# Moving 38 on-chip transposes from TensorE to the DMA queue in a layernorm, linear attention and SwiGLU kernel

## The chip, the cores and the metric

The kernel runs on one core of a Trainium2 chip. The metric is the device time of one execution in microseconds (us); 306.36 us is the median of the three runs shown for the kernel before. Engines are named as in the profile: PE (TensorE, matrix multiply; PEld is its weight load), ACT (ScalarE), DVE (VectorE), POOL (GpSimd), SP (SyncE, which here does nothing but issue DMAs).

## What is computed

S = 2048 tokens of D = 640 features, 32 heads of 20 features, F = 1536. Everything is bfloat16 at the borders.

```python
xn = _layernorm(x, axis=-1)
return x + _A_ref(xn, A_wqkv, A_w_phi, A_wo) + _B_ref(xn, B_w1, B_w3, B_w2)

# _A_ref
q, k, v = qkv[0], qkv[1], qkv[2]                  # from x @ wqkv
pq = jnp.einsum("bhsd,hdf->bhsf", q, w_phi)
pk = jnp.einsum("bhsd,hdf->bhsf", k, w_phi)
phi_q = jnp.concatenate([_softmax(pq, axis=-1), _softmax(-pq, axis=-1)], axis=-1)
phi_k = jnp.concatenate([_softmax(pk, axis=-1), _softmax(-pk, axis=-1)], axis=-1)
kv = jnp.einsum("bhsf,bhsd->bhfd", phi_k, v)
z  = jnp.einsum("bhsf->bhf", phi_k)
num = jnp.einsum("bhqf,bhfd->bhqd", phi_q, kv)
den = jnp.einsum("bhqf,bhf->bhq", phi_q, z)[..., None] + 1e-6
o = num / den                                     # then (B, S, D) @ wo

# _B_ref
h = _silu(gate) * up                              # gate = x @ w1, up = x @ w3
out = jnp.einsum("bsf,fd->bsd", h, w2)
```

## The kernel before

The tokens are cut into T = 16 tiles of 128, and into 4 blocks of 512 for the products that keep 512 tokens in the free dimension. A matmul contracts over the 128 partitions, so the features must lie on the partitions: DC = 5 chunks of 128 make up D. All operands stay in SBUF.

The steps, by the names in the code and the tiles that the profile shows:

- `loads` issues all early DMAs on SP, in one list: token tiles into `x_tok`, `wv`, the k part and the q part of `wqkv` into `wqk_s`, `phi_s`, and `w1_s`, `w3_s` in three slices each (the profile calls these two and `w2_s` `w_s`).
- `ln_stats` (DVE BN_STATS and BN_AGGR, then POOL for the power -0.5) and `ln_apply` (DVE or ACT) normalise `x_tok` in place. `xn_transpose` turns one tile: five PE transposes (matmuls against `ident`, seen as `PS<-ident,x_tok`) into one PSUM bank, and one copy by ACT or DVE into `xnT`.
- `fold_t` transposes one 128-column strip of wk or wq in the same way (`PS<-ident,wqk_s`, five per strip, five strips per weight) into `wqkT`; `fold_mm` multiplies it with the block diagonal of w_phi (`BDc`) into `Wkp` or `Wqp`, so that no separate feature-map product is needed later. One call of `fold_mm` is six matmuls.
- `v_tile` and `k_tile` are ten matmuls of 320 columns each per token tile; `k_tile` is followed by two exponentials on ACT into `ekt`. `k_norm` divides them by their sums: a sum and a reciprocal on DVE (`S64`, `rS64`), two multiplications on POOL, which write `ekt` again.
- `kv_sum` sums over all 16 token tiles: ten groups of 16 matmuls (`PS<-v,ekt`), each followed on DVE and POOL by the masking into `KVc`. It needs the last `k_norm`.
- `q_proj` (five matmuls of 512 columns and two exponentials into `EqT`), then `q_tok` per token tile: 12 matmuls against `KVc`, two small ACT copies, and six DVE operations up to `o_tok`, which has three buffers. `o_transpose` turns `o_tok` into `oT`: five PE transposes (`PS<-ident,o_tok`) and a copy.
- `mlp` is one of 48 units (4 blocks of 12): ten matmuls of 512 columns, a tanh on ACT, two DVE operations (`t1`, `hT`). `out_tile` is 34 matmuls of 320 columns per token tile (`wo_s`, `w2_s`), an addition on DVE (`xres`), and a store.

The order is set by a planner that runs when the program is built. Six streams (`norms`, `attention`, `k_norms`, `o_transposes`, `mlps`, `outs`) each offer their next step; for each the planner works out from its own costs when the step could start, and takes the earliest. What it takes is appended to the lists of the engines, and at run time each engine goes through its list in order, waiting on semaphores. So a step that was planned for a certain moment holds up everything behind it on the same engine if its data come later. The steps of `attention` win ties over those of `mlps`. A DMA in the plan holds SP for 0.06 us and moves at a fixed rate.

Parts of SBUF are used twice: `hT3` and `w2_s` lie on `ekt`, so block 3 of `mlps` waits in the plan until `kv_sum` is done; `hT2` lies on `x_tok`; `oT` lies on `v2`; `KVc`, `prod` and `o_tok` lie on `wqkT`.

The comparison that picks the next step:

```python
            if any(o.eng == "PE" for o in ops):
                at = max(P.ready(ops), P.free["PE"] + 0.15)
            else:
                at = P.start_of(ops[0])
                if i == 0 and at < P.free["PE"] + 2.0:
                    at = -1.0
            if best is None or at < best[0]:
                best = (at, i, ops, after)
```

Of the kernel before, what the change touches and what calls it, by code (L numbers as in the profile page):

```python
# [9 lines left out]
D = 640  # L10
# [4 lines left out]
DC = D // 128  # L15
# [27 lines left out]
class _Program:  # L43
# [60 lines left out]
        self.pending.append(o)  # L104
        return o

    def dma(self, eng, out, in_):
        m = self.eng[eng].dma_start
        nbytes = 1
        for n in out.shape:  # L110
            nbytes *= n
        nbytes *= mybir.dt.size(out.dtype)
        o = _Op(eng, lambda: m(out, in_), self.regions(in_), self.regions(out), nbytes, True)  # L113
        o.name = "dma:" + out.name
        self.pending.append(o)
        return o
# [123 lines left out]
def bass_parallel_sum__linear_kernel_hedgehog__glu_gated_swiglu__prompt_kernel(  # L240
# [11 lines left out]
    bf = DT.bfloat16  # L252
    f32 = DT.float32
    P = _Program(nc)
# [6 lines left out]
    def region(size):  # L261
        o = top[0]
        top[0] = o + (size + 31) // 32 * 32
        assert top[0] <= arena_size, top[0]
        return a0 + o

    def new(name, shape, dtype, offset=None):
        size = mybir.dt.size(dtype)
        for n in shape[1:]:
            size *= n  # L270
        return P.sbuf(name, shape, dtype, region(size) if offset is None else offset)
# [15 lines left out]
    xnT = new("xnT", [128, DC, S], bf)  # L287
# [8 lines left out]
    x_tok = new("x_tok", [128, T, D], bf, RX)  # L296
# [12 lines left out]
    RE = region(40960)  # L309
# [1 line left out]
    hT3 = new("hT3", [128, FC, 512], bf, RE)  # L311
    w2_s = new("w2_s", [128, FC, D], bf, RE + 12288)
    EqT1 = new("EqT1", [128, 2, DC, 512], bf, RE + 27648)
    wqk_s = new("wqk_s", [128, DC, 2 * D], bf, RE + 40960 - 12800)
    hT = [hT0, hT1, hT2, hT3]

    RV = region(21504)
# [1 line left out]
    oT = new("oT", [128, DC, S], bf, RV)  # L319
# [4 lines left out]
    wqkT = new("wqkT", [128, 2 * DC, D], bf, RW)  # L324
    KVc = new("KVc", [128, 2, DC, 8 * 22], bf, RW)
    prod = new("prod", [128, 2, 2, D], bf, RW + 3520)
    o_tok = new("o_tok", [128, 3, D], bf, RW + 8640)
# [3 lines left out]
    PSb = PS[:].bitcast(bf)  # L331
# [14 lines left out]
    def tr(o, i, idn=None):  # L346
        idn = ident[:] if idn is None else idn
        P.op("PE", "transpose", [o], [i, idn], (o, i, idn), cost=0.06)

    def free(ap):  # L350
        n = 1
        for s in ap.shape[1:]:
            n *= s
        return n
# [13 lines left out]
    def copy(eng, o, i, fast=1):  # L368
        if eng == "ACT":
            act(o, i, ACT.Copy)  # L370
        else:
            P.op(eng, "tensor_copy", [o], [i], (o, i), cost=0.14 + free(o) / 960 / fast)

    def evac(o, i):

        a = P.free["ACT"] + 0.17 + free(o) / 1200
        d = P.free["DVE"] + 0.14 + free(o) / 960 / (2 if i.dtype == bf else 1)
        copy("ACT" if a <= d else "DVE", o, i, 2 if i.dtype == bf else 1)
# [12 lines left out]
    wqkv_t = A_wqkv.rearrange("(c p) n -> p c n", p=128)  # L391
# [4 lines left out]
    def loads():  # L396
        def x(a, b):
            P.dma("SP", x_tok[:, a:b, :], x_t[:, a:b, :])

        def w13(a, b):  # L400
            P.dma("SP", w1_s[:, :, a:b], w1_t[:, :, a:b])
            P.dma("SP", w3_s[:, :, a:b], w3_t[:, :, a:b])

        x(0, 1)
        x(1, 2)
        P.dma("SP", wv[:], wqkv_t[:, :, 2 * D:3 * D])
        x(2, 4)
        P.dma("SP", wqk_s[:, :, D:2 * D], wqkv_t[:, :, D:2 * D])
        P.dma("SP", phi_s[:], phi_t)
        x(4, 8)  # L410
        w13(0, 512)
        x(8, 12)
        P.dma("SP", wqk_s[:, :, 0:D], wqkv_t[:, :, 0:D])
        w13(512, 1024)
        x(12, 16)
        w13(1024, 1536)
# [40 lines left out]
    def xn_transpose(t, k):  # L457
        for dc in range(DC):
            tr(PSb[:, k * 1024 + 128 * dc:k * 1024 + 128 * dc + 128],
               x_tok[:, t, 128 * dc:128 * dc + 128])  # L460
        src = PSb[:, k * 1024:k * 1024 + D].rearrange("p (c n) -> p c n", n=128)
        evac(xnT[:, :, t * 128:(t + 1) * 128], src)


    def block_diag():
        for c in range(DC):
# [2 lines left out]
            tt("POOL", BDc[:, c, 0:n * DH].rearrange("p (h k) -> p h k", k=DH),  # L469
               phi_s[:, c, :].unsqueeze(1).to_broadcast([128, n, DH]),  # L470
               GM[:, c, h0:h1 + 1].unsqueeze(2).to_broadcast([128, n, DH]), ALU.mult)

    def fold_t(which, e, k):
        for dc in range(DC):
            tr(PSb[:, k * 1024 + 128 * dc:k * 1024 + 128 * dc + 128],
               wqk_s[:, dc, which * D + 128 * e:which * D + 128 * e + 128])
        evac(wqkT[:, which * DC + e, :], PSb[:, k * 1024:k * 1024 + D])

    def fold_mm(which, dc, k):
        first = [True, True]  # L480
# [92 lines left out]
           g.unsqueeze(3).to_broadcast([128, 4, 16, DH]), ALU.mult)  # L573
        tt("DVE", o_tok[:, t % 3, :], p2[:, 0, :], p2[:, 1, :], ALU.add, 2)

    def o_transpose(t, k):
        for dc in range(DC):
            tr(PSb[:, k * 1024 + 128 * dc:k * 1024 + 128 * dc + 128],
               o_tok[:, t % 3, 128 * dc:128 * dc + 128])
        src = PSb[:, k * 1024:k * 1024 + D].rearrange("p (c n) -> p c n", n=128)  # L580
        evac(oT[:, :, t * 128:(t + 1) * 128], src)


    nmlp = [0]

# [13 lines left out]
    def load_xres(t):  # L599
        P.dma("SP", xres[:, t % 4, :], x_t[:, t, :])  # L600
# [15 lines left out]
    def banks(n):  # L616

        def free_at(k):
            return max([o.end for i in range(k, k + n) for o in P.bank.get(("P", i), {}).values()],
                       default=0.0)  # L620
        return min(range(0, 8, n), key=free_at)
# [33 lines left out]
    def transposed(t):  # L655
        while done["ln"] <= t:
            yield None
        yield lambda: xn_transpose(t, banks(1))
        done["t"] = t + 1

    def attention():
        yield from transposed(0)
        for t in range(4):
            if t < 3:
                yield from transposed(t + 1)
            yield lambda t=t: v_tile(t, banks(2))
        for e in range(DC):
            yield lambda e=e: fold_t(1, e, banks(1))
        for dc in range(DC):
            yield lambda dc=dc: fold_mm(1, dc, banks(2))  # L670
        for t in range(T):
            yield lambda t=t: k_tile(t, banks(2))
            done["k"] = t + 1
            if 2 <= t < 14:
                yield from transposed(t + 2)
            if t >= 4:
                yield lambda t=t: v_tile(t, banks(2))
            if 4 <= t < 9:
                yield lambda e=t - 4: fold_t(0, e, banks(1))
            if 9 <= t < 14:  # L680
                yield lambda dc=t - 9: fold_mm(0, dc, banks(2))
        yield lambda: P.dma("SP", wo_s[:], A_wo.rearrange("(c p) d -> p c d", p=128))
        for fc in range(DC):
            yield lambda fc=fc: q_proj(0, fc, banks(1))
        while done["n"] < T:
            yield None
        for fc in range(DC):
            for sg in range(2):
                yield lambda fc=fc, sg=sg: kv_sum(sg, fc, banks(1))
        done["kv"] = 1  # L690
        yield lambda: P.dma("SP", w2_s[:], B_w2.rearrange("(c p) d -> p c d", p=128))
        yield lambda: (load_xres(0), load_xres(1))
        for b in range(NB):
            for j in range(4):
                t = 4 * b + j
                yield lambda t=t: q_tok(t, banks(4))
                done["q"] = t + 1
                if b + 1 < NB:
                    for fc in range((5 * j + 3) // 4, (5 * j + 8) // 4):
                        yield lambda b=b, fc=fc: q_proj(b + 1, fc, banks(1))  # L700

    def o_transposes():
        for t in range(T):
            while done["q"] <= t:
                yield None
            yield lambda t=t: o_transpose(t, banks(1))
            done["o"] = t + 1

    def mlps():
# [14 lines left out]
    n = len(streams)  # L724
    heads, alive = [None] * n, [True] * n
    while any(alive):
        best = None
        for i in range(n):
            if heads[i] is None and alive[i]:
                s = next(streams[i], StopIteration)  # L730
                if s is StopIteration:
                    alive[i] = False
                else:
                    heads[i] = s
            if heads[i] is None:
                continue
            save = nmlp[0], len(finish)
            ops = P.step(heads[i])
            after = nmlp[0], finish[save[1]:]
            nmlp[0] = save[0]  # L740
            del finish[save[1]:]
            if any(o.eng == "PE" for o in ops):
                at = max(P.ready(ops), P.free["PE"] + 0.15)
            else:
                at = P.start_of(ops[0])
                if i == 0 and at < P.free["PE"] + 2.0:
                    at = -1.0
            if best is None or at < best[0]:
                best = (at, i, ops, after)
        if best is None:  # L750
            continue
        at, i, ops, after = best
        nmlp[0] = after[0]
        finish.extend(after[1])
        P.commit(ops)
        heads[i] = None
# [61 lines left out]
```

## Time and profile before

| what | value |
|---|---|
| time, three runs | 305.68, 306.36, 308.53 us; median 306.36 us |
| time of the profiled execution | 307.55 us |
| span of its instructions | 305.8 us (1.75 us of the time lie around it) |
| PE | 286.2 us busy, 94% of the span, 2066 matmuls |
| DVE, ACT, POOL | 191.6, 118.4, 59.1 us busy |
| mean granted TensorE clock | 0.988 of full speed |

The span is the time from the first to the last instruction on the chip. Matmuls overlap in the profile, since their ends are modelled: the time that a group really takes is the distance from its start to the start of the next group on PE, and not its own duration. The share of busy time is a mean over stages with different limits, so the rows further below go stage by stage.

### The profile page before, as it was taken

The page shows a single profiled execution, that of the slowest core. Times are in us where ns is not written, and L with a number is a line of the kernel's source. Part 1 is how long each engine was busy: PE and PEld are TensorE (multiplying, and loading weights), DVE is VectorE, ACT ScalarE, POOL GpSimd, SP SyncE. Part 2 cuts the span into 40 slices and gives each one's busy share as a digit, 9 for nine tenths or more (in the row PEclk, how much of TensorE's full clock was granted, in tenths as well). Part 3 has the DMA queues.
Part 4 walks back from the last instruction along what each step waited for, and adds up shares of the span by engine and source line. Part 5 has one row for each costly group of instructions (what it writes and reads, how often), then busy time and mean ns, then how long its engine had stood idle before and what let it go on. Part 6 is the DMA issues. An engine that isn't in the chain of part 4 may idle for free.

```text
span 305.8 us, 4978 instructions
## 1 busy us (share of the span) xinstructions
PE 286.2 (94%) x2066; PEld 181.9 (59%) x2066; DVE 191.6 (63%) x335; ACT 118.4 (39%) x212; POOL 59.1 (19%) x90
## 2 busy tenths in 40 slices
PE   0699999999999999999659999999999999999995
PEld 0476777775444444444359555555667777777773
DVE  3758888889566656565734699799546675511212
ACT  2277989868522232323100565556323311200000
POOL 4431646898800000000061000000000000000000
PEclk9999999999999999999968999999999999999999
DMA  7998000030000000000000810000101221122121
GB/s 230 340 355 260 2 1 2 1 109 0 2 0 0 0 2 0 1 2 0 0 0 2 263 62 0 2 1 2 43 0 45 58 73 45 61 70 86 43 66 43
DMA packets 15543, 17.38 MB, mean 57 GB/s; under 512 B 1441, under 2 KB 15521, under 8 KB 15521
## 3 DMA queue, kind: packets, MB, share of 16 engines
q1 hardware_dynamic: 15520, 17.07, 17.5%
q8 instruction: 16, 0.26, 0.4%
q14 instruction: 7, 0.05, 0.1%
HBM read 14.44 MB, written 2.62 MB: 56 GB/s over the span
## 4 chain that ended last, share of the span: by engine, by line
PE 92%; DVE 3%; DMA 2%; POOL 1%; ACT 1%; issue 0%; SPq 0%
PE PS L101 92%; DMA x_tok<-in_A_x_dram 2%; POOL ekt L101 1%; DVE prod L101 0%; DVE S_61 L101 0%; SPq L113 0%; ACT EqT_81 L101 0%; DVE bst L101 0%; DVE xres L101 0%; DVE t_68 L101 0%; ACT th L101 0%; DVE den_s L101 0%; DVE rS_62 L101 0%; DVE x_tok L101 0%; ACT e_s L101 0%
## 5 line engine op out<-in xcount | busy, mean ns | idle before, releaser
L101 PE MATMUL PS<-xnT,w_s 128*128 128x512 bf16 x480 | 105.7, 379 | 0.0
L101 PEld LDWEIGHTS PS<-xnT,w_s 128*128 128x128 bf16 x480 | 46.4, 98 | 54.1 <-ACT EqT_75 L101 0.3
L101 ACT ACTIVATE th<-PS 128x512 f32<-128x512 f32 x48 | 28.8, 601 | 75.0 <-PE PS L101 75.0
L101 POOL TENSOR_TENSOR ekt<-ekt,rS_62 128x640 bf16<-128x640 bf16 x32 | 39.7, 1273 | 78.8 <-DVE rS_62 L101 78.7
L101 DVE SCALAR_TENSOR_TENSOR t_68<-th,PS 128x512 bf16<-128x512 f32 x48 | 32.9, 685 | 31.0 <-ACT th L101 30.9
L101 DVE TENSOR_TENSOR xres<-PS,xres 128x640 bf16<-128x640 f32 x16 | 13.2, 825 | 48.5 <-PE PS L101 48.5
L101 PE MATMUL PS<-wv,xnT 128*128 128x320 bf16 x160 | 26.3, 316 | 0.0
L101 PE MATMUL PS<-wo_s,oT 128*128 128x320 bf16 x160 | 24.6, 299 | 0.8 <-ACT EqT_81 L101 0.8
L101 DVE TENSOR_REDUCE S_61<-ekt 128x64 f32<-128x1280 bf16 x16 | 23.3, 1455 | 1.7 <-ACT ekt L101 1.7
L101 DVE TENSOR_TENSOR prod<-PS,g_s 128x1280 bf16<-128x1280 f32 x16 | 23.9, 1491 | 0.5
L101 PE MATMUL PS<-Wkp,xnT 128*128 128x320 bf16 x160 | 24.0, 299 | 0.0
L101 PE MATMUL PS<-xnT,Wqp 128*128 128x512 bf16 x100 | 23.7, 379 | 0.0
L101 ACT ACTIVATE ekt<-PS 128x640 bf16<-128x640 f32 x32 | 20.8, 705 | 7.2 <-PE PS L101 7.1
L101 ACT ACTIVATE e_s<-PS 128x64 f32<-128x64 f32 x32 | 9.1, 283 | 37.3 <-PE PS L101 36.3
L101 PEld LDWEIGHTS PS<-wv,xnT 128*128 128x128 bf16 x160 | 16.0, 104 | 6.2
L101 PEld LDWEIGHTS PS<-wo_s,oT 128*128 128x128 bf16 x160 | 15.1, 98 | 7.1 <-ACT EqT_81 L101 1.0
L101 PE MATMUL PS<-v_83,ekt 128*128 128x147 bf16 (+1 forms) x160 | 13.9, 259 | 5.7 <-POOL ekt L101 5.7
L101 DVE BATCH_NORM_STATS2 bst<-x_tok 128x6 f32<-128x320 bf16 x32 | 15.3, 477 | 5.6 <-DMA x_tok<-in_A_x_dram 5.0
L101 PEld LDWEIGHTS PS<-Wkp,xnT 128*128 128x128 bf16 x160 | 15.2, 98 | 5.3
L101 PEld LDWEIGHTS PS<-v_83,ekt 128*128 128x128 bf16 x160 | 13.5, 113 | 6.3 <-POOL ekt L101 6.0
L101 PE MATMUL PS<-ident,x_tok 128*128 128x128 bf16 x80 | 7.9, 236 | 9.4 <-DVE x_tok L101 9.4
L101 PEld LDWEIGHTS PS<-xnT,Wqp 128*128 128x128 bf16 x100 | 9.4, 98 | 8.8
(65 smaller groups left out, 325.1 us busy)
## 6 DMA issues: line engine op xcount, KB each, us to landing
w_s<-in_B_w_dram SPq DMA_DIRECT2D x6, 640.0 KB, 10.2
xres<-in_A_x_dram SPq DMA_DIRECT2D x16, 160.0 KB, 2.4
out_dram<-xres SPq DMA_DIRECT2D x16, 160.0 KB, 1.8
x_tok<-in_A_x_dram SPq DMA_DIRECT2D x3, 640.0 KB, 9.0
w_s<-in_B_w_dram SPq DMA_DIRECT2D x1, 1920.0 KB, 8.1
wqk_s<-in_A_wqkv_dram SPq DMA_DIRECT2D x2, 800.0 KB, 9.2
wv<-in_A_wqkv_dram SPq DMA_DIRECT2D x1, 800.0 KB, 5.9
wo_s<-in_A_wo_dram SPq DMA_DIRECT2D x1, 800.0 KB, 4.6
```

Source lines behind the costliest of these rows:

```text
L101: o = _Op(eng, lambda: m(*args, **kw), r, w, cost)
```

## The change

Three kinds of transposes leave PE and become DMAs with a transpose, issued by SP: those of the normalised token tiles 4 to 15 (`x_tok` to `xnT`, SBUF to SBUF), those of the attention output (`o_tok` to `oT`, SBUF to SBUF, all 16 tiles), and those of wk and wq, which are now read from DRAM straight into `wqkT` in one DMA of 800 KB each; `wqk_s` and `fold_t` are gone. Token tiles 0 to 3 are still transposed on PE. With each PE transpose goes its copy out of PSUM. Besides, steps of the stream `k_norms` are planned as if they could start 4 us earlier than they can.

```diff
-    def dma(self, eng, out, in_):
-        m = self.eng[eng].dma_start
+    def dma(self, eng, out, in_, transpose=False):
+        m = self.eng[eng].dma_start_transpose if transpose else self.eng[eng].dma_start
...
-        P.dma("SP", wqk_s[:, :, D:2 * D], wqkv_t[:, :, D:2 * D])
         P.dma("SP", phi_s[:], phi_t)
+        P.dma("SP", wqkT[:, DC:2 * DC, :], A_wqkv[:, D:2 * D], True)
         x(4, 8)
         w13(0, 512)
         x(8, 12)
-        P.dma("SP", wqk_s[:, :, 0:D], wqkv_t[:, :, 0:D])
+        P.dma("SP", wqkT[:, 0:DC, :], A_wqkv[:, 0:D], True)
...
-        yield lambda: xn_transpose(t, banks(1))
+        if t < 4:
+            yield lambda: xn_transpose(t, banks(1))
+        else:
+            yield lambda: P.dma("SP", xnT[:, :, t * 128:(t + 1) * 128], x_tok[:, t, :], True)
...
-        for e in range(DC):
-            yield lambda e=e: fold_t(1, e, banks(1))
...
-            if 4 <= t < 9:
-                yield lambda e=t - 4: fold_t(0, e, banks(1))
...
-            yield lambda t=t: o_transpose(t, banks(1))
+            yield lambda t=t: P.dma("SP", oT[:, :, t * 128:(t + 1) * 128], o_tok[:, t % 3, :], True)
...
                 at = P.start_of(ops[0])
+                if i == 2:
+                    at -= 4.0
```

The plan comes out in another order on every engine. Four places matter below.

First, PE behind the last `v_tile` of tiles 0 to 3 (`wv`). `PS<-ident,wqk_s` is `fold_t`, `PS<-BDc,wqkT` is `fold_mm`, `PS<-xnT,w_s` is `mlp`, `PS<-Wkp,xnT` is `k_tile`. Before:

```order
L101 MATMUL PS<-wv,xnT 128x320 x20
L101 MATMUL PS<-ident,wqk_s 128x128 x25
L101 MATMUL PS<-xnT,w_s 128x512 x10
L101 MATMUL PS<-BDc,wqkT 128x140 x2
L101 MATMUL PS<-BDc,wqkT 128x80 x2
L101 MATMUL PS<-BDc,wqkT 128x140 x4
```

And now:

```order
L101 MATMUL PS<-wv,xnT 128x320 x20
L101 MATMUL PS<-BDc,wqkT 128x140 x2
L101 MATMUL PS<-BDc,wqkT 128x80 x2
L101 MATMUL PS<-BDc,wqkT 128x140 x4
...
L101 MATMUL PS<-BDc,wqkT 128x140 x2
L101 MATMUL PS<-Wkp,xnT 128x320 x40
L101 MATMUL PS<-xnT,w_s 128x512 x50
```

The 30 matmuls of `fold_mm` now stand directly behind `wv`, with no unit of `mlp` between them and `k_tile`; the first five units come behind four `k_tile`.

Second, PE around `kv_sum` (`PS<-v,ekt`), behind the last `v_tile`. Before:

```order
L101 MATMUL PS<-wv,xnT 128x320 x10
L101 MATMUL PS<-xnT,Wqp 128x512 x25
L101 MATMUL PS<-xnT,w_s 128x512 x330
L101 MATMUL PS<-v_83,ekt 128x147 x64
L101 MATMUL PS<-v_83,ekt 128x168 x32
L101 MATMUL PS<-v_83,ekt 128x147 x64
```

And now:

```order
L101 MATMUL PS<-wv,xnT 128x320 x10
L101 MATMUL PS<-xnT,Wqp 128x512 x25
L101 MATMUL PS<-xnT,w_s 128x512 x10
L101 MATMUL PS<-v_82,ekt 128x147 x64
L101 MATMUL PS<-v_82,ekt 128x168 x32
L101 MATMUL PS<-v_82,ekt 128x147 x64
```

One unit of `mlp` stands ahead of `kv_sum` instead of 33; the others follow it, beside `q_tok`.

Third, SP, the queue of DMAs, up to the first store. Before:

```order
L113 DMA x_tok<-in_A_x_dram 128x2x640
L113 DMA wqk_s<-in_A_wqkv_dram 128x5x640
L113 DMA phi_s<-in_A_w_phi_dram 128x5x20
L113 DMA x_tok<-in_A_x_dram 128x4x640
L113 DMA w_s<-in_B_w_dram 128x5x512 x2
```

And now:

```order
L113 DMA phi_s<-in_A_w_phi_dram 128x5x20
L113 DMA_TRANSPOSE wqkT<-in_A_wqkv_dram 128x5x640
L113 DMA x_tok<-in_A_x_dram 128x4x640
...
L113 DMA w_s<-in_B_w_dram 128x5x512 x2
L113 DMA_TRANSPOSE xnT<-x_tok 128x5x128 x12
L113 DMA wo_s<-in_A_wo_dram 128x5x640
L113 DMA w_s<-in_B_w_dram 128x12x640
L113 DMA xres<-in_A_x_dram 128x640 x2
L113 DMA_TRANSPOSE oT<-o_tok 128x5x128 x16
```

The transposed wk stands ahead of token tiles 4 to 7; the 12 transposes of token tiles stand behind all early loads and ahead of those of `wo_s` and `w2_s`, the 16 of the attention output behind these.

Fourth, DVE and ACT while wk is folded. DVE (from the last statistics of tiles 4 to 7) and ACT (from the copies of the last two of the first four `v_tile`) before:

```order
L101 BN_AGGR mv<-bst 128x2
L101 COPY wqkT<-PS 128x640 x3
L101 SCALAR_TENSOR_TENSOR t_68<-th,PS 128x512
L101 SCALAR_TENSOR_TENSOR hT_76<-t_68,PS 128x512
...
L101 ACTIVATE v_83<-PS 128x32x20 x2
L101 ACTIVATE x_tok<-x_tok,rstd 128x640
L101 ACTIVATE wqkT<-PS 128x640 x2
L101 ACTIVATE th<-PS 128x512
L101 ACTIVATE x_tok<-x_tok,rstd 128x640
L101 ACTIVATE Wkp<-PS 128x640 x3
```

And now:

```order
L101 BN_AGGR mv<-bst 128x2
L101 CAST Wkp<-PS 128x640 x2
L101 TENSOR_SCALAR x_tok<-x_tok,mv,rstd 128x640
...
L101 ACTIVATE v_82<-PS 128x32x20 x2
L101 ACTIVATE x_tok<-x_tok,rstd 128x640
L101 ACTIVATE Wkp<-PS 128x640 x3
L101 ACTIVATE x_tok<-x_tok,rstd 128x640 x2
```

Two of the five copies into `Wkp` now stand on DVE directly behind the statistics of tiles 4 to 7, and three on ACT directly behind the `ln_apply` of tile 4; the copies into `wqkT` and the units of `mlp` that stood there are gone.

## Rows read from the trace of the kernel before

**Rows 1.** The page: the chain that ended last, by engine

```profile
PE 92%; DVE 3%; DMA 2%; POOL 1%; ACT 1%; issue 0%; SPq 0%
```

**Rows 2.** Stretches of 10 us: busy PE, PEld, DVE, ACT, POOL; clock; DMA

```profile
150.00:160.00 10.00, 4.30 (x39) 3.97 (x37) 5.41 (x9) 0.00 (x0) 5.32 (x6) 0.77 0.00 0
160.00:170.00 10.00, 10.00 (x124) 9.41 (x122) 3.99 (x16) 0.00 (x0) 1.73 (x8) 0.89 0.04 4
...
220.00:230.00 10.00, 8.64 (x77) 6.01 (x76) 6.00 (x10) 4.29 (x10) 0.00 (x0) 1.00 0.07 17
```

**Rows 3.** PE in order of time: start us, duration us, group

```profile
19.00 1.56 PE L101 MATMUL PS<-ident,wqk_s 128*128 128x128 bf16 x25
20.39 2.32 PE L101 MATMUL PS<-xnT,w_s 128*128 128x512 bf16 x10
...
57.12 0.48 PE L101 MATMUL PS<-BDc,wqkT 128*128 128x140 bf16 x6
57.43 1.52 PE L101 MATMUL PS<-Wkp,xnT 128*128 128x320 bf16 x10
58.79 0.44 PE L101 MATMUL PS<-ident,x_tok 128*128 128x128 bf16 x5
59.07 1.52 PE L101 MATMUL PS<-wv,xnT 128*128 128x320 bf16 x10
```

**Rows 4.** PE in order of time around the sum over keys

```profile
149.42 1.06 PE L101 MATMUL PS<-v_83,ekt 128*128 128x147 bf16 x14
153.96 0.24 PE L101 MATMUL PS<-v_83,ekt 128*128 128x147 bf16 x1 [3.48 <-POOL ekt L101]
156.41 12.59 PE L101 MATMUL PS<-v_83,ekt 128*128 128x147 bf16 x145 [2.21 <-POOL ekt L101]
```

**Rows 5.** DVE in order of time, late in the same stretch

```profile
168.00 0.30 DVE L101 TENSOR_TENSOR KVc<-PS,GM 128x140 bf16<-128x140 f32 x1 [0.51 <-PE PS L101]
...
169.04 0.30 DVE L101 TENSOR_TENSOR KVc<-PS,GM 128x140 bf16<-128x140 f32 x1 [0.51 <-PE PS L101]
```

**Rows 6.** The page: key normalise on POOL (busy us, mean ns | idle before, releaser)

```profile
L101 POOL TENSOR_TENSOR ekt<-ekt,rS_62 128x640 bf16<-128x640 bf16 x32 | 39.7, 1273 | 78.8 <-DVE rS_62 L101 78.7
```

**Rows 7.** DVE and ACT in order of time around the fold of wk

```profile
13.05 1.02 DVE L101 BATCH_NORM_STATS2 bst<-x_tok 128x6 f32<-128x320 bf16 x2 [0.17 <-DMA x_tok<-in_A_x_dram]
...
17.49 0.21 DVE L101 BATCH_NORM_AGGREGATE mv<-bst 128x2 f32<-128x12 f32 x1
...
19.80 0.91 ACT L101 ACTIVATE x_tok<-x_tok,rstd 128x640 bf16<-128x640 bf16 x1
...
23.07 1.91 ACT L101 ACTIVATE Wkp<-PS 128x640 bf16<-128x640 f32 x3
```

**Rows 8.** The page: DMA busy in 40 slices of 7.65 us; one queue; two groups of issues

```profile
DMA  7998000030000000000000810000101221122121
...
q1 hardware_dynamic: 15520, 17.07, 17.5%
...
xres<-in_A_x_dram SPq DMA_DIRECT2D x16, 160.0 KB, 2.4
...
wqk_s<-in_A_wqkv_dram SPq DMA_DIRECT2D x2, 800.0 KB, 9.2
```

**Rows 9.** PE and DVE in order of time beside the attention of single tiles

```profile
200.28 4.48 PE L101 MATMUL PS<-xnT,w_s 128*128 128x512 bf16 x20
204.59 0.85 PE L101 MATMUL PS<-KVc,EqT_81 128*128 128x154 bf16 x12
205.28 1.24 PE L101 MATMUL PS<-xnT,Wqp 128*128 128x512 bf16 x5
...
205.80 0.22 DVE L101 TENSOR_TENSOR pr_s<-e_s 128x64 f32<-128x64 f32 x1
...
208.87 0.68 DVE L101 SCALAR_TENSOR_TENSOR t_68<-th,PS 128x512 bf16<-128x512 f32 x1
...
210.18 0.22 DVE L101 TENSOR_TENSOR pr_s<-e_s 128x64 f32<-128x64 f32 x1
```

More of the change, by code (lines that the diff above doesn't have):

```diff
@@ L313, in bass_parallel_sum__linear_kernel_hedgehog__glu_gated_swiglu__prompt_kernel @@
     EqT1 = new("EqT1", [128, 2, DC, 512], bf, RE + 27648)
-    wqk_s = new("wqk_s", [128, DC, 2 * D], bf, RE + 40960 - 12800)
     hT = [hT0, hT1, hT2, hT3]
@@ L471, in block_diag @@
                GM[:, c, h0:h1 + 1].unsqueeze(2).to_broadcast([128, n, DH]), ALU.mult)
[L473 to L477, printed above, removed]
     def fold_mm(which, dc, k):
@@ L574, in q_tok @@
         tt("DVE", o_tok[:, t % 3, :], p2[:, 0, :], p2[:, 1, :], ALU.add, 2)
[L576 to L581, printed above, removed]
     nmlp = [0]
```

## The prediction, made before the changed kernel ran

> **What bounds the kernel now.** I read the chain that ended last first: 92% of it is PE [rows 1], so what leaves PE's list leaves the time, as long as nothing new is waited for. Next the stretches of 10 us, to see where PE was not full: of those that this change can touch, 150 to 170, where PE is busy for 4.30 of the first 10 us and the clock then stands at 0.77 and 0.89, and 220 to 230, with 1.36 us missing [rows 2]. Last the order of time on PE, because matmul durations overlap there: a group is priced from its start to the next start. In [rows 3] five transposes of a token tile take 59.07 - 58.79 = 0.28 us although 0.44 is printed, and 25 of wk take 1.39 us, again 0.28 per five. One `fold_mm` takes 0.31 us and one `k_tile` 1.36 us.
>
> **Transposes leave PE.** 12 token tiles, 16 tiles of attention output and 10 strips of wk and wq: 38 groups of five at 0.28 us, **-10.6 us**, all on the path, since PE is full around them. I take the attention groups at the price of the others. Their 38 copies on ACT and DVE go too; I count nothing for them, because those engines are not the bound there.
>
> **Key normalise first.** In [rows 4] `kv_sum` begins at 149.42 and ends at 156.41 + 12.59 = 169.00: 19.6 us. Two waits for POOL's `ekt`, 3.48 and 2.21 us, are in it, and behind them matmuls at the lower clock. At full clock a group of 16 takes 1.04 us (from one `KVc` to the next [rows 5]); eight of these and two of 168 columns, estimated at 1.04 x 168/147 = 1.19, make 10.7 us. So the waits and the clock cost 8.9 us. The cause is no lack of POOL time: POOL sat idle for 78.7 us until DVE's `rS` came [rows 6], because the planner put unit after unit of `mlp` ahead of the last two `k_norm` on DVE. With the bonus of 4 us they go in as soon as their exponentials are done. POOL needs 2 x 1.27 = 2.55 us per tile [rows 6], PE at least 2 x 1.36 = 2.72 us for `k_tile` and `v_tile` [rows 3], so POOL keeps pace; and after the last `v_tile` PE still has 25 matmuls of `q_proj` and one unit of `mlp`, together some 7.5 us at 0.215 us per matmul [rows 9], ahead of `kv_sum`. The last tile needs a sum, a reciprocal and 2.55 us of POOL, about 5 us. I book **-8.9 us**; bounds are -8.9 and, if the wait reappears in full, 0.
>
> The two short waits of 220 to 230, 1.4 us, lie among output tiles that are mixed with `q_tok`; these tiles now come at the very end, in one piece. **-1.4 us**.
>
> **The fold of wk loses its cover.** Before, three units of `mlp` ran between the folds; now `k_tile` follows at once, and needs all five chunks of `Wkp`. PE arrives at 19.00 [rows 3], and 5 x 0.31 + 1.36 would bring it to 21.9 at the end of the first `k_tile`. On ACT three of the copies stand behind the `ln_apply` of tile 4, which began at 19.80 and took 0.91; three copies took 1.91 [rows 7]: the last chunk is there at 22.6. So 1.0 us is waited, up to 1.9 if PE cannot use the early chunks. I take **+1.5 us**. This holds if tiles 4 to 7 land about when they do now (DVE began their statistics at 13.05, ended at 17.7 [rows 7]); they now queue behind the transposed wk, and I estimate 2 to 3 us of slack, since ACT did not wait for the statistics. After such a wait the clock may drop as it did around 156: 19.6 - 10.7 - 5.7 = 3.2 us at most, from waits longer than this one; I take 0.
>
> **The price of a transposing DMA.** No row shows one. Lower bound: that of a plain transfer of the same bytes, 2.4 us to landing for 160 KB, and for 800 KB the 9.2 us of wk and wq now, most of it queueing [rows 8]; then nothing moves. Upper bound from the packets: 15520 of them took 17.5% of 16 engines' 305.8 us [rows 8], 55 ns each. A plain 800 KB load is 640 packets of 1280 B, 2.2 us on 16 engines. If every run of 128 elements (256 B, the length written per feature and token tile) cost a packet of its own, 160 KB would take 640 packets, 2.2 us, and 800 KB 3200 packets, 11.0 us, 8.8 more than now. I take the plain end: the bytes are the same and that row is the nearest. Nothing waits for 2.4 us here: a token tile's transpose is needed one `k_tile` later than the five units of `mlp` which stand ahead of tile 4, and an `o_tok` buffer comes round after three tiles.
>
> The Trainium skill contradicts itself on this. Advanced Engine Details and Errata, section X-Bar Transpose (TRN2), says that such DMAs are as fast as regular ones, by which the sum would stay as it is. VectorE: DVE Perf Modes, section The three transpose paths, gives 1309 ns for 128x128 by DMA against 390 ns by TensorE and advises TensorE where PSUM will do; if that were time in series, the sum would be that of the slow rival below. No row here shows the DMA; for TensorE the trace has 0.28 us for five in a row, far under that figure.
>
> SP issues in order, and the new DMAs stand in its list: the 12 of the token tiles ahead of `wo_s` and `w2_s`, the 16 of the attention output ahead of the third `xres` load. All of these are used only by the output tiles at the end, so I cost the order at 0.
>
> **DVE becomes the limit for four tiles.** The 35 units of `mlp` that are left run beside `q_tok`. Of a tile, DVE needs 208.87 - 205.80 = 3.07 us for the attention and 1.31 us per unit [rows 9]; PE 0.69 us for `q_tok` and 2.16 per unit (4.31 for two). In blocks 0 to 2 the new order has seven units and five `q_proj` per four tiles: PE 4 x 0.69 + 7 x 2.16 + 5 x 1.08 = 23.3 us, DVE 4 x 3.07 + 7 x 1.31 = 21.5. PE leads. (1.08 is five matmuls of 512 columns at the unit's rate.) In block 3 there is no `q_proj`, and each tile stands with two units: PE 5.00, DVE 5.69. Four tiles at 0.7 us: **+2.8 us**; bounds 0 (the PSUM buffers let PE run ahead) and 6 (waits on the single operations as well).
>
> **Sum.** 305.8 - 10.6 - 8.9 - 1.4 + 1.5 + 2.8 = 289.2 us of span, a change of 16.6 us. The profiled execution took 307.55 us, 1.75 around its span and 1.2 above the median of the runs; I set the change against the median: 306.4 - 16.6 = 289.8, rounded to **290**.
>
> **Rivals.** (a) *A packet for every 256 B.* Tiles 4 to 7 land 8.8 us later, the last `Wkp` comes at about 29 and the fold waits 6 us more. Early loads, which end near 30.6 (four of 40 slices [rows 8]), then end near 48, so tile 4 is transposed at 51, while PE would reach its `k_tile` at 22.9 + 3 x 1.36 + 5 x 2.16 + 6 = 44: 7 more. 290 + 13 = 303, say 302. For it: the xnT runs are that short. Against: nothing in the trace.
>
> (b) *The crossbar moves 128x128 blocks one after the other*, slower than before. Its price per block lies between 0.44 us (a fifth of 2.2) and 2.4 us (a whole small transfer [rows 8]); at 1 us, wk takes 25 us and a token tile 5. The fold then waits 20 us more; the loads end near 76, tile 4 comes at 82 against PE at 58, 24 more; and 11 further tiles at 5 us against PE's 11 x 2.72 + 6 x 2.16 + 5 x 0.31 = 44 cost 11. 290 + 55 = 345. It is slower than before from 2.4 us of ring time per 160 KB on, where the two waits make 16.5 us. For it: five blocks per tile are five separate transposes on PE too. Against: 16 engines work on every transfer of the trace. By the page's 1309 ns this case would give some 370 us; this sentence carries nothing else.
>
> (c) *DVE sets the pace through all of `q_tok`.* PE leads in blocks 0 to 2 by only 1.8 us per four tiles; if small gaps between dependent DVE operations of 0.8 us per tile count there, 12 tiles cost some 7 us after that lead: 297. For it: no output tile dilutes these stretches any more.
>
> (d) *The change doesn't end the wait for `ekt`*: the bonus is spent on other tiles, POOL comes late and the clock falls, 290 + 8.9 = 299. Against: 7.5 us of other work on PE stand ahead of `kv_sum`, against about 5.
>
> **Chances and range.** Forecast 0.60, (a) 0.12, (b) 0.08, (c) 0.13, (d) 0.07. The forecast's own range is 285 to 296: 3.2 us for the clock, 1.5 for the fold and 3 for DVE either way. It reaches up to 302 to take in (c), (d) and half of (a). About 1% is what a measurement here can tell from no change, so faster means under 303.3 and slower over 309.4: faster 0.86 (all but (b) and the upper part of (a)), same 0.06, slower 0.08.
>
> **What would show it.** Right: PE with 42 - 38 = 4 groups of transposes; no wait for POOL at `kv_sum`, now before 110, and no fall of the clock there; the wait of a microsecond or two on PE near 21, released by ACT or DVE; transposes landing in 2 to 3 us; PE waiting for DVE only in the last tiles of `q_tok`. Wrong: PE waiting for a DMA into `xnT` or `wqkT`, or `x_tok` tiles 4 to 7 landing well after 16.

## The result, and the profile after

The changed kernel takes 286.56 us (median of 4 runs, 286.34 to 287.10) against 307.33 us for the kernel before beside it (4 runs, 305.68 to 308.53): a ratio of 0.933, 95% interval 0.9276 to 0.9384. The profiled execution took 286.44 us; its span is 284.4 us, 21.4 less than before, and its mean granted clock is 1.0. The prediction was 290.0 (285 to 302) with 16.6 us off the span.

From the page of the changed kernel: busy time, the queue, the chain by engine, and key normalise on POOL (answering to [rows 1, 6, 8]).

```profile
PE 270.4 (95%) x1859; PEld 167.8 (59%) x1876; DVE 181.7 (64%) x317; ACT 107.3 (38%) x192; POOL 60.0 (21%) x90
...
q1 hardware_dynamic: 39488, 21.66, 29.2%
...
PE 89%; DVE 5%; DMA 2%; issue 1%; ACT 1%; SPq 0%
...
L101 POOL TENSOR_TENSOR ekt<-ekt,rS_62 128x640 bf16<-128x640 bf16 x32 | 40.1, 1276 | 19.0 <-DVE rS_62 L101 19.0
```

PE is still the bound, with 1859 matmuls in the records instead of 2066. By the code there are 190 fewer, 1876; the other 17 are missing in the records, and each of them leaves an empty place of about 0.05 us in PE's busy time, which is no wait. POOL's idle time ahead of key normalise fell from 78.8 us [rows 6] to 19.0: the work is the same (40.1 us), it is only done earlier. The queue carries 39488 packets instead of 15520, and 21.66 MB instead of 17.07: the 28 transposes of 160 KB inside SBUF are 4.59 MB.

Stretches of 10 us of the changed kernel, columns as in [rows 2]. The sum over keys is now near 90; 180 to 190 is the last block of `q_tok`.

```profile
90.00:100.00 10.00, 10.00 (x145) 9.65 (x144) 5.37 (x18) 0.32 (x1) 1.72 (x9) 1.00 0.01 2
...
180.00:190.00 10.00, 9.60 (x61) 4.88 (x61) 9.55 (x19) 3.52 (x8) 0.00 (x0) 1.00 0.09 18
190.00:200.00 10.00, 9.86 (x46) 4.31 (x45) 9.60 (x17) 2.59 (x5) 0.00 (x0) 1.00 0.24 49
...
220.00:230.00 10.00, 10.00 (x76) 7.19 (x75) 1.65 (x2) 0.00 (x0) 0.00 (x0) 1.00 0.22 67
```

PE in order of time in the changed kernel: the head and the fold, the sum over keys, the last `q_tok`.

```profile
14.30 2.88 PE L101 MATMUL PS<-wv,xnT 128*128 128x320 bf16 x20
17.02 1.45 PE L101 MATMUL PS<-BDc,wqkT 128*128 128x140 bf16 x24
19.38 0.49 PE L101 MATMUL PS<-BDc,wqkT 128*128 128x140 bf16 x6 [0.91 <-ACT Wkp L101]
19.70 5.60 PE L101 MATMUL PS<-Wkp,xnT 128*128 128x320 bf16 x40
...
90.61 10.83 PE L101 MATMUL PS<-v_82,ekt 128*128 128x147 bf16 x160
...
183.24 0.85 PE L101 MATMUL PS<-KVc,EqT_81 128*128 128x154 bf16 x12
183.93 4.49 PE L101 MATMUL PS<-xnT,w_s 128*128 128x512 bf16 x19
188.50 0.86 PE L101 MATMUL PS<-KVc,EqT_81 128*128 128x154 bf16 x12
189.62 17.70 PE L101 MATMUL PS<-xnT,w_s 128*128 128x512 bf16 x79 [0.26 <-DVE t_68 L101]
```

Six places give the balance. `kv_sum` takes 10.83 us without a wait, where it took 156.41 + 12.59 - 149.42 = 19.6 [rows 4]: -8.8. The 38 groups of transposes are gone: -10.6. The stretch 220 to 230 is full: -1.4. The fold takes 19.70 - 17.02 = 2.68 us where five calls of 0.31 would take 1.55: +1.1. The first four `v_tile` end at 17.02 instead of 19.00 [rows 3]: -2.0, which was in no term. PE loses 0.9 us in the last block: from its first `q_tok` at 173.22 to the first `out_tile` at 207.16 it is 33.94 us, where four `q_tok` at 0.69 us and 14 units of `mlp` at 2.16 make 33.0: +0.9. Ahead of that, from the first `q_tok` of all at 103.43 to 173.22, PE loses nothing: 12 `q_tok`, 15 `q_proj` at 1.08 us and 21 units make 69.84 us, and 69.79 pass; the 0.05 us that stretches there lack are missing records. Together -20.8, against -21.4 measured; 0.6 us stays unassigned. Most of it may be four of the 16 groups of `o_tok`, which took 0.39 or 0.40 us before and not 0.28, as this one on PE:

```profile
243.15 0.44 PE L101 MATMUL PS<-ident,o_tok 128*128 128x128 bf16 x5
243.54 1.53 PE L101 MATMUL PS<-wo_s,oT 128*128 128x320 bf16 x10
```

DVE and ACT of the changed kernel in order of time (the statistics of tiles 2 and 3, those of tiles 4 to 7, the copies into `Wkp`), answering to [rows 7]:

```profile
7.68 1.02 DVE L101 BATCH_NORM_STATS2 bst<-x_tok 128x6 f32<-128x320 bf16 x2 [1.99 <-DMA x_tok<-in_A_x_dram]
...
13.29 1.02 DVE L101 BATCH_NORM_STATS2 bst<-x_tok 128x6 f32<-128x320 bf16 x2 [1.25 <-DMA x_tok<-in_A_x_dram]
...
18.63 1.98 ACT L101 ACTIVATE Wkp<-PS 128x640 bf16<-128x640 f32 x3
```

SP's own queue in order of time, where the duration is how long the issue holds SP:

```profile
3.27 5.45 SPq L113 DMA_TRANSPOSE wqkT<-in_A_wqkv_dram  x1
8.77 0.57 SPq L113 DMA_DIRECT2D x_tok<-in_A_x_dram  x1
...
11.38 8.25 SPq L113 DMA_TRANSPOSE wqkT<-in_A_wqkv_dram  x1
```

And the DMA issues by group, with the median time from issue to landing:

```profile
oT<-o_tok SPq DMA_TRANSPOSE x16, 2.6
xnT<-x_tok SPq DMA_TRANSPOSE x12, 2.6
```

A 160 KB transpose inside SBUF lands in 2.6 us against 2.4 for a plain load of that size from DRAM [rows 8], and no matmul of the changed kernel waits for one.

### The profile page after: what moved, and what is told of

Same layout as the page of the kernel before. It is cut to its first block, busy times and chain, and to the rows that moved or that the text cites. A ratio compares the mean times of both kernels' runs of the same rounds, so it can differ in the third digit from the quotient of the medians.

```text
span 284.4 us, 4567 instructions
## 1 busy us (share of the span) xinstructions
PE 270.4 (95%) x1859; PEld 167.8 (59%) x1876; DVE 181.7 (64%) x317; ACT 107.3 (38%) x192; POOL 60.0 (21%) x90
## 2 busy tenths in 40 slices
DMA packets 39509, 21.95 MB, mean 77 GB/s; under 512 B 26688, under 2 KB 39488, under 8 KB 39488
## 3 DMA queue, kind: packets, MB, share of 16 engines
q1 hardware_dynamic: 39488, 21.66, 29.2%
## 4 chain that ended last, share of the span: by engine, by line
PE 89%; DVE 5%; DMA 2%; issue 1%; ACT 1%; SPq 0%
PE PS L101 89%; DMA x_tok<-in_A_x_dram 2%; DVE prod L101 2%; DVE t_68 L101 1%; DVE den_s L101 1%; DVE hT_79 L101 1%; SPq L113 0%; DVE bst L101 0%; DVE xres L101 0%; ACT x_tok L101 0%; ACT v_82 L101 0%; DVE g_s L101 0%; DVE hT_71 L101 0%; ACT Wkp L101 0%; DVE pr_s L101 0%
## 5 line engine op out<-in xcount | busy, mean ns | idle before, releaser
L101 POOL TENSOR_TENSOR ekt<-ekt,rS_62 128x640 bf16<-128x640 bf16 x32 | 40.1, 1276 | 19.0 <-DVE rS_62 L101 19.0
L101 PE MATMUL PS<-wv,xnT 128*128 128x320 bf16 x160 | 25.4, 309 | 0.0
L101 PE MATMUL PS<-xnT,Wqp 128*128 128x512 bf16 x95 | 22.6, 379 | 0.3
L101 PEld LDWEIGHTS PS<-wo_s,oT 128*128 128x128 bf16 x160 | 15.7, 98 | 6.2
L101 ACT ACTIVATE v_82<-PS 128x640 bf16<-128x640 f32 x16 | 11.3, 707 | 7.3 <-PE PS L101 6.7
L101 PE MATMUL PS<-w_s,hT_76 128*128 128x320 bf16 x96 | 13.7, 299 | 0.0
L101 PE MATMUL PS<-w_s,hT_77 128*128 128x320 bf16 x96 | 13.7, 299 | 0.0
```

Of the source, the lines that this page charges most:

```text
L101: o = _Op(eng, lambda: m(*args, **kw), r, w, cost)
```

## The experiments

The theory is the sum of the prediction: each part brings its own term, whatever the others do. Its rival is that the parts need each other. The kernel before, run beside each group of experiments, took 306.42 us (median of 8 runs) for e1, e2, e4 and e5, 306.64 (15 runs) for e3 and e6 to e8, 306.71 (11 runs) for e9 to e11, and 306.72 (11 runs) for e12. Ratios are against these, with their 95% intervals.

### e1_bonus: the kernel before with the bonus alone

```diff
                 at = P.start_of(ops[0])
+                if i == 2:
+                    at -= 4.0
```

> The kernel before with the 4 us bonus of the key normalise alone; all transposes stay on PE. If the terms of the prediction simply add, the wait for POOL's ekt and the slow matmuls behind it go (8.9 us) and nothing else: about 298 us, no wait of PE for POOL at the sum over keys. Rival: the units of mlp that now run beside the attention of single tiles meet the copies of the transposes on ACT and DVE and wait there: 300 to 303 us.

Measured: 301.84 us, ratio 0.985 (0.9825 to 0.9876), span 300.3. The wait for `ekt` is gone here too, so the bonus does its work by itself; but only 4.6 of the 10 us arrive. PE in order of time shows where the rest went:

```profile
182.96 0.44 PE L101 MATMUL PS<-ident,o_tok 128*128 128x128 bf16 x5
184.20 4.49 PE L101 MATMUL PS<-xnT,w_s 128*128 128x512 bf16 x19 [0.80 <-ACT oT L101]
```

Behind five transposes of `o_tok`, the next unit of `mlp` waits for ACT's copy out of PSUM. In all, PE waits 2.6 us for copies into `oT` (3 times) and 1.3 us for those into `v`. The kernel before has neither wait. With the fold of wk beginning at 19.77 instead of 19.00 [rows 3] the profiles close: -8.8 - 1.4 + 3.9 + 0.8 = -5.5 us, and the spans are 305.8 and 300.3. The rival is right: the new order needs the copies gone.

### e2_nobonus: the changed kernel without the bonus

```diff
-                if i == 2:
-                    at -= 4.0
```

> The changed kernel without the bonus; all transposes that the change moves are DMAs. If the terms add, the wait at the sum over keys comes back whole, 8.5 to 8.9 us: about 295 us. Rival, that the two halves of the change depend on each other: without the bonus nearly all units of mlp are used up ahead of the sum over keys, the attention of the last tiles then runs with nothing beside it, PE waits about 2.7 us for DVE's prod at three or four tiles, and output tiles wait for a transpose by DMA at the end: about 300 us.

Measured: 309.45 us, ratio 1.013 (1.0074 to 1.0187), a little slower than before; span 306.0, mean clock 0.978. All three sets of transposes by DMA, with 10.6 us less work on PE, lose 3 us. Both theories were too kind. PE waits 5.7 us for `ekt`, as before, 6.0 us for `prod` of DVE and 4.7 us for one `oT`. PE, DVE and SP, each in order of time:

```profile
242.54 0.86 PE L101 MATMUL PS<-KVc,EqT 128*128 128x154 bf16 x12 [2.28 <-DVE prod L101]
...
251.69 0.49 DVE L101 TENSOR_TENSOR o_tok<-prod 128x640 bf16<-128x640 bf16 x1
...
287.95 0.34 SPq L113 DMA_DIRECT2D out_dram<-xres  x1
288.74 2.52 SPq L113 DMA_TRANSPOSE oT<-o_tok  x2
...
291.77 2.40 PE L101 MATMUL PS<-wo_s,oT 128*128 128x320 bf16 x10 [4.71 <-DMA oT<-o_tok]
```

DVE has the last `o_tok` ready at 252.2, but the transposes of the last two tiles are issued only from 288.74 on, more than 36 us later. No transpose was slow: SP issues in order, and in this plan these two stand behind output stores, each of which waits for an addition on DVE that follows the matmuls of its own tile (the store at 287.95 for the addition at 287.10). The 10 matmuls of `wo_s` behind the wait take 293.96 - 291.77 = 2.19 us instead of 1.36. Stretches of 10 us show both places and their clock:

```profile
240.00:250.00 10.00, 3.96 (x35) 2.69 (x33) 9.38 (x22) 1.58 (x6) 0.00 (x0) 0.72 0.36 82
...
290.00:300.00 10.00, 8.23 (x49) 5.44 (x50) 0.82 (x1) 0.00 (x0) 0.00 (x0) 0.83 0.18 33
```

In 240 to 250 the last tiles of `q_tok` stand alone, with no unit of `mlp` left to run beside them, because those were spent ahead of `kv_sum`: DVE is busy for 9.38 us of ten and PE for 3.96. With the bonus the units follow `kv_sum`, and all 16 transposes of `o_tok` are issued ahead of the first store.

### e3_weights, e4_tokens, e5_output: one set of transposes each, without the bonus

Each is the kernel before with one part of the change's diff: the two loads of wk and wq with `fold_t` removed (e3), `xn_transpose` of tiles 4 to 15 (e4), `o_transpose` (e5).

```diff
+        P.dma("SP", wqkT[:, DC:2 * DC, :], A_wqkv[:, D:2 * D], True)      # e3
+            yield lambda: P.dma("SP", xnT[:, :, t * 128:(t + 1) * 128], x_tok[:, t, :], True)      # e4
+            yield lambda t=t: P.dma("SP", oT[:, :, t * 128:(t + 1) * 128], o_tok[:, t % 3, :], True)      # e5
```

> The kernel before with wk and wq alone transposed by DMA from DRAM. Terms that add: 10 x 0.28 = 2.8 us less, 1 us more for the fold, and the 2 us by which the first value tiles ended earlier in the changed kernel, which should show here too if it comes from the loads: about 303 us, first statistics of tiles 2 and 3 near 7.7 instead of 8.5. Rival, that this head start comes from something else in the change: 305 us and 8.5.

> The kernel before with token tiles 4 to 15 alone transposed by DMA. Terms that add: 12 x 0.28 = 3.4 us less, about 303.5 us, PE waiting for no DMA into xnT. Rival: the transposes queue behind the early loads and PE waits at the keys of tile 4; then no gain or a loss.

> The kernel before with the attention output alone transposed by DMA. If the terms add: 16 x 0.28 = 4.5 us less, about 302.5 us. Rival, dependence on the bonus: with the order of before the planner places the last attention tiles back to back and an output tile behind a DMA that has just been issued; PE waits for prod and for the DMA, and the gain is lost: 306 to 309 us.

Measured: e3 307.21 us (1.0026, 0.9999 to 1.0053), e4 303.13 (0.9893, 0.9854 to 0.9931), e5 313.35 (1.0231, 1.0196 to 1.0266). Only e4 does what its own term says (-3.3 us against 12 x 0.28 = 3.4). In e3 the plan came out with three late `k_norm` instead of two, as PE in order of time shows:

```profile
151.50 0.30 PE L101 MATMUL PS<-v,ekt 128*128 128x147 bf16 x1 [3.55 <-POOL ekt L101]
153.95 0.30 PE L101 MATMUL PS<-v,ekt 128*128 128x147 bf16 x1 [2.15 <-POOL ekt L101]
156.41 12.23 PE L101 MATMUL PS<-v,ekt 128*128 128x147 bf16 x145 [2.15 <-POOL ekt L101]
```

That is 7.8 us of waits where [rows 4] have 5.7, and the fold waits 0.91 us for ACT's `Wkp`, as in the changed kernel; so the 2.8 us saved are gone. The statistics of tiles 2 and 3 do begin at 7.74, but the fold at 18.21 and not at 17.02. In e5 the sum of PE's waits shows the two new ones of e2, beside those for `ekt`:

```profile
PE PS L101 <- DVE prod L101: 4.5, 2, 2.3
PE PS L101 <- DMA oT<-o_tok: 3.9, 1, 3.9
```

They cost more than the 4.5 us that 16 groups free, and the mean clock falls to 0.972. So the same edit that is worth 6.9 us in the next experiment costs 6.9 us here.

### e9_output_pe, e10_tokens_pe, e11_weights_pe: the changed kernel with one set back on PE

```diff
-            yield lambda t=t: P.dma("SP", oT[:, :, t * 128:(t + 1) * 128], o_tok[:, t % 3, :], True)
+            yield lambda t=t: o_transpose(t, banks(1))      # e9
-        if t < 4: ... else: P.dma("SP", xnT[...], x_tok[:, t, :], True)
+        yield lambda: xn_transpose(t, banks(1))             # e10
-        P.dma("SP", wqkT[:, DC:2 * DC, :], A_wqkv[:, D:2 * D], True)
+        P.dma("SP", wqk_s[:, :, D:2 * D], wqkv_t[:, :, D:2 * D])   # e11, ahead of phi; wq alike, and fold_t
```

> The changed kernel with the 16 transposes of the attention output back on PE, each with its copy by ACT or DVE; everything else as changed. Theory A (a transpose costs only PE's own 0.28 us): 16 x 0.28 = 4.5 us, 286.6 + 4.5 = 291.1. Theory B (the copies count too, since PE waits for the ACT or DVE copy that empties the PSUM bank or queues behind other work, as in the kernel with the bonus alone, whose trace has 2.6 us of PE waits released by ACT oT): 286.6 + 4.5 + 2.6 = 293.7, and the trace shows waits released by ACT or DVE oT.

> The changed kernel with the transposes of token tiles 4 to 15 back on PE. Theory A: 12 x 0.28 = 3.4 us, 290.0. Theory B: the copies make PE wait as well, as in the kernel with the bonus alone (1.3 us of PE waits released by ACT v, windows of 10 us with PE at 9.2 to 9.4 between 50 and 80): 291.5 or more.

> The changed kernel with wk and wq loaded plainly and turned on PE. Theory A: 10 x 0.28 = 2.8 us of PE, less the 1.05 us of the wait in the fold that goes: 288.4. Theory B: the head of 2.0 us that the changed kernel gained, because token tiles 2 and 3 landed earlier with wk's load behind phi, is lost as well: 290.4, with the first fold work at about 19.0 instead of 17.0 and the statistics of tiles 2 and 3 at 8.5 instead of 7.7.

Measured: 293.46 us (0.9574, 0.9541 to 0.9607), 291.67 (0.9504, 0.9474 to 0.9534) and 290.27 (0.9458, 0.9427 to 0.9489). Theory B holds three times. Against 286.56 the parts are worth 6.9, 5.1 and 3.7 us, 15.7 together; from e1 to the changed kernel it is 301.84 - 286.56 = 15.3. With the bonus in place the parts do add up, each with more than its own 0.28 us per group. In e9, PE and ACT in order of time:

```profile
176.25 0.44 PE L101 MATMUL PS<-ident,o_tok 128*128 128x128 bf16 x5
177.49 4.49 PE L101 MATMUL PS<-xnT,w_s 128*128 128x512 bf16 x20 [0.80 <-ACT oT L101]
...
176.11 0.63 ACT L101 ACTIVATE e_s<-PS 128x64 f32<-128x64 f32 x2 [0.83 <-PE PS L101]
176.73 0.70 ACT L101 ACTIVATE oT<-PS 128x640 bf16<-128x640 bf16 x1
```

ACT's copy stands behind the two `e_s` of the tile whose 12 matmuls ran just before, and takes 0.70 us; the next unit of `mlp` waits for it, 0.80 us. This happens for three tiles: 16 x 0.28 + 3 x 0.80 = 6.9 us, the difference of the medians. In e10 a copy into `xnT` stands on ACT behind two `ln_apply`, and `k_tile` waits for it:

```profile
65.76 1.53 PE L101 MATMUL PS<-Wkp,xnT 128*128 128x320 bf16 x10 [0.44 <-ACT xnT L101]
...
63.33 1.78 ACT L101 ACTIVATE x_tok<-x_tok,rstd 128x640 bf16<-128x640 bf16 x2
64.95 0.75 ACT L101 ACTIVATE xnT<-PS 128x640 bf16<-128x640 bf16 x1
```

With this wait of 0.44 us, another of 0.16 us for a copy into `v`, and a first fold at 17.61 instead of 17.02, 12 x 0.28 = 3.4 becomes 4.6 of the 4.9 us between the spans. For e11 the next experiment looks at the head.

### e12_phi_first: the load of phi ahead of the plain load of wk

```diff
-        P.dma("SP", wqk_s[:, :, D:2 * D], wqkv_t[:, :, D:2 * D])
         P.dma("SP", phi_s[:], phi_t)
+        P.dma("SP", wqk_s[:, :, D:2 * D], wqkv_t[:, :, D:2 * D])
```

> The kernel with wk and wq on PE (290.3 us), with one edit: the load of phi is issued ahead of the plain load of wk instead of behind it, as the changed kernel has it; the lists of PE are the same. Theory A (token tiles 2 and 3 land earlier in the changed kernel because of the order of the issues): their statistics begin near 7.8 us instead of 8.5 to 9.2, and the time falls by 0.5 to 1 us to about 289.5. Theory B (they land earlier because the transposing load behind them takes less from them than a plain load does): no change, 290.3, statistics at 8.5 to 9.2.

Measured: 289.28 us (0.9459, 0.9423 to 0.9495) against 290.27 for e11. The first work behind the four `v_tile`, on PE, in e11 and then in e12:

```profile
19.53 1.56 PE L101 MATMUL PS<-ident,wqk_s 128*128 128x128 bf16 x25
```

```profile
17.80 1.56 PE L101 MATMUL PS<-ident,wqk_s 128*128 128x128 bf16 x25
```

The profiles lean to theory A, by 1.73 us, and the statistics of tiles 2 and 3 begin at 8.31 instead of 9.19, between the two theories; the times do not settle it, since their intervals lie on each other. In e4, whose loads are issued in the order of the kernel before up to there, these statistics begin at 7.74 and the first work of this kind at 16.92. Over all profiles this moment scatters: 17.02 to 18.42 (mean 17.66) in the eight kernels with wk by transposing DMA, 16.92 to 19.77 (mean 18.80) in the five with wk by a plain DMA ahead of phi. So 1.1 us of the 2.0 belong to the change as a mean, and the rest to where this one pair of executions fell in the scatter. Which of the two causes it is stays open.

### e6_extra_plain, e7_extra_crossbar: the price of a transposing load

Both are the changed kernel with one more load of the 800 KB of wk, behind the transposed wk and ahead of token tiles 4 to 7, into a buffer that nothing reads; e6 plain, e7 transposed.

```diff
         P.dma("SP", wqkT[:, DC:2 * DC, :], A_wqkv[:, D:2 * D], True)
+        P.dma("SP", dum[:], wqkv_t[:, :, D:2 * D])              # e6
+        P.dma("SP", dum[:], A_wqkv[:, D:2 * D], True)           # e7
```

> The changed kernel with one plain 800 KB load more (the k part of wqkv into a buffer that nobody reads), behind the transposed wk and ahead of token tiles 4 to 7. All theories: their statistics on DVE begin 2.2 to 2.4 us later than 13.3, since 800 KB pass at some 350 GB/s; this is the yardstick for the next run.

> As the run with the plain extra load, but the extra 800 KB are transposed. If each 256 B are a packet of 20 ns (what the counts of the two traces give), 3200 packets on 16 engines take 4 us: tiles 4 to 7 come 4 us later than 13.3. If a packet cost 55 ns, as the prediction's upper bound had it: 11 us later. If transposes are as fast as plain loads: 2.2 to 2.4 us, as in the plain run.

Measured: 286.61 and 287.46 us (one run each), spans 284.8 and 285.6. The statistics of tiles 4 to 7, which wait for the loads behind the extra one, and the queue; e6, then e7 (there also the statistics of tiles 2 and 3, and SP's own queue):

```profile
15.85 1.02 DVE L101 BATCH_NORM_STATS2 bst<-x_tok 128x6 f32<-128x320 bf16 x2 [0.64 <-DMA x_tok<-in_A_x_dram]
...
q1 hardware_dynamic: 40144, 22.48, 31.1%
```

```profile
8.57 1.02 DVE L101 BATCH_NORM_STATS2 bst<-x_tok 128x6 f32<-128x320 bf16 x2 [2.82 <-DMA x_tok<-in_A_x_dram]
...
18.67 1.02 DVE L101 BATCH_NORM_STATS2 bst<-x_tok 128x6 f32<-128x320 bf16 x2 [2.60 <-DMA x_tok<-in_A_x_dram]
...
q1 hardware_dynamic: 42720, 22.48, 32.1%
...
9.66 3.92 SPq L113 DMA_TRANSPOSE dum<-in_A_wqkv_dram  x1
13.62 0.58 SPq L113 DMA_DIRECT2D x_tok<-in_A_x_dram  x1
```

Against 13.29 in the changed kernel the plain load delays them by 2.56 us and the transposed one by 5.38. In e7 the statistics of tiles 2 and 3, whose load is ahead of the extra one, are already 0.89 us later than in the changed kernel (7.68), and in e6 0.11. Without this the extra loads cost 2.4 and 4.5 us, so the transposed one costs nearly twice as much. It has 42720 - 39488 = 3232 packets, the plain one 656: a packet for every 256 B, as rival (a) supposed, but 4.5 us over 16 engines make 22 ns of delay for each, not 55; of the three expectations the 4 us at 20 ns are nearest. Most of the delay is there before the load of tiles 4 to 7 is issued: SP issues it at 13.62 instead of 8.77, because the extra issue holds SP for 3.92 us and the one ahead of it for 6.33 instead of 5.45. Whether SP is held by the making of the packets or by engines that have not caught up, these runs do not show. The Trainium skill, Advanced Engine Details and Errata, section X-Bar Transpose (TRN2), says that such DMAs are as fast as regular ones; the landing of 160 KB (2.6 against 2.4 us) agrees, the 800 KB from DRAM do not. Even the 5.38 us hardly move the time: the plan has other work for PE meanwhile.

### e8_pool_add: a version that might beat the changed kernel

The changed kernel with the last addition of the attention, into `o_tok`, on POOL instead of DVE.

```diff
-        tt("DVE", o_tok[:, t % 3, :], p2[:, 0, :], p2[:, 1, :], ALU.add, 2)
+        tt("POOL", o_tok[:, t % 3, :], p2[:, 0, :], p2[:, 1, :], ALU.add)
```

> The changed kernel with the last addition of the attention of a tile (prod into o_tok) on POOL instead of DVE, 0.4 us off DVE per tile. If DVE limits PE in the last four tiles, their distance on PE falls from 5.0 to 5.3 us to 5.0 and the four waits of the trace (about 0.9 us) go: 285.6 us, 0.3% less. If these waits are PE's own, or POOL's longer addition comes on the path: 286.6 us or more.

Measured: 287.30 us (285.70 to 287.72, 5 runs), ratio 0.9354 (0.9324 to 0.9384), no different from the changed kernel. The limit by DVE is gone from PE's order of time, where the tiles of the last block now stand 5.01 us apart (5.26 for the last pair of the changed kernel), with no wait, and PE loses nothing from the first tile of the block to the first `out_tile`:

```profile
178.16 0.85 PE L101 MATMUL PS<-KVc,EqT 128*128 128x154 bf16 x12
183.17 0.85 PE L101 MATMUL PS<-KVc,EqT 128*128 128x154 bf16 x12
```

What it removes, 0.9 us, is no more than the scatter; this profile's fold began at 18.42 instead of 17.02, which hides more than that.

## Why the prediction was right, and where it was not

The total came out 3.4 us under the forecast and within the range; the mechanism of each large term is in the trace, but the terms do not stand by themselves, as the sum treated them.

**Transposes leave PE, -10.6.** Right against the kernel before, where no copy made PE wait. "Their 38 copies on ACT and DVE go too; I count nothing for them" failed as a step: in the order that the bonus makes, the copies are worth 3 to 4 us (e1: 3.9 us of waits for `oT` and `v`; e9 and e10: 2.4 and 0.6). The bonus raises this cost and the DMAs remove it, so it does not show in the difference of the two kernels. The price taken for the attention groups, 0.28 us, holds for most; four of the 16 took 0.39 or 0.40.

**Key normalise first, -8.9 and -1.4.** Measured -8.8 and -1.4 in their places. The cause was named rightly: POOL's work is the same and its idle time went from 78.8 to 19.0 us. But e1 shows that the bonus alone brings 4.6 us, not 10.3, since the copies take the rest back.

**SP's order, 0.** Right by luck: only the bonus made it so. The reason given ("used only by the output tiles at the end") looked at when the data are needed, and not at what stands ahead in the queue. In e2 and e5 a transpose stands on SP behind stores that wait for DVE, and PE waits 4.7 and 3.9 us for it.

**The fold, +1.5.** Measured +1.1, of which 0.91 is a wait for ACT's `Wkp`. The engine and the copy are those described, the place is not: the last call of `fold_mm` waits, which does not read `Wkp` and so can only want the PSUM bank that the copy empties; `k_tile` then waits for nothing. (The upper bound, 1.9, is 22.6 + 1.36 - 21.9 = 2.1 by its own figures.) Tiles 4 to 7 came at 13.29 against 13.05 [rows 7], within the slack assumed.

**The price of the DMA, taken as plain.** For 160 KB 2.6 against 2.4 us, right; for 800 KB nearly twice a plain load (e6, e7), wrong in size and without effect. That such an issue holds SP for microseconds was not thought of.

**DVE in block 3, +2.8.** Mis-sized: 0.9 us, of which 0.26 is a wait that the trace puts down to DVE; e8, with less work on DVE, has none of the 0.9. The sum compared busy times per tile as if PE could not run ahead. PE did run ahead, which was the lower bound named there: DVE is still busy for 9.60 us of the ten from 190 to 200, behind the last `q_tok`.

**Not in the sum: the head, -2.0.** Tiles 2 and 3 landed at 7.68 instead of 8.52, and the four `v_tile` ended 2.0 us earlier; 1.1 us of it as a mean over the profiles. This and the two terms that were too large (0.4 and 1.9) make 4.3 us, against a miss of 4.8 in the span.

Of the rivals, (a) had the packets right and their price at more than twice the measured one; (b) is out, at 1.2 us of issue and 2.6 to landing for five blocks; (c) and (d) did not come: PE loses nothing beside `q_tok` in blocks 0 to 2, and `kv_sum` waits for nothing. (The price of (c) does not follow from its figures: 12 x 0.8 - 3 x 1.8 is 4.2 us, not 7.)

## What to carry to other kernels

A transpose on PE can cost more than its matmuls where ACT or DVE is in demand: look for waits on PE that are released by the copy out of PSUM, and test the offload in the order in which it will run, since here the same edit was worth 6.9 us with one order and cost 6.9 with another. Before a DMA is put on an in-order queue, list what is ahead of it there and what that waits for, above all stores. When a change has several parts, one kernel with each part alone and one with each part left out tell whether their terms may be added.

## What the runs showed of the hardware

An issue with transpose holds SP far longer than a plain one: 1.20 us for 160 KB, 5.45 and 8.25 us for 800 KB while other loads run, 3.92 in e7, against 0.43 to 0.57 for most plain loads. An extra 800 KB from DRAM moves the same bytes either way (22.48 MB in all in e6 and in e7), transposed in packets of 256 B, and delays what is behind it by 4.5 us instead of 2.4. And a wait of 4.71 us near the end of e2 is followed by matmuls that take 2.19 us instead of 1.36 for ten. The stretch of 10 us around them has a mean granted clock of 0.83; in the two pieces of 2 us from 292 to 296 it is 0.57 and 0.58, near the lower of its two levels (1.2 of 2.4 GHz), and in the next 1.00. So such a wait costs PE more than its own length.
